# Ordering a fused attention and Fourier-mixing kernel anew: slots in twos, new durations in the order's model, an earlier copy of the mask factors

## The chip, the cores and the metric

The kernel runs on one core of one Trainium2 chip. The metric is the device time in microseconds (us) of one execution. "TensorE" is the matrix engine (PE in the profile, PEld its weight loads), "VectorE" is DVE, "ScalarE" is ACT, "GpSimd" is POOL and "SyncE" (SP) issues most of the DMAs (454 of the 459 in the profile before). PSUM is the memory of the four pools in which this kernel keeps TensorE's results; a "bank" is one result's room in such a pool.

## The reference

```python
# B, H, S, D = 4, 8, 768, 64; d_model = H*D = 512; blocks of 32
scores = scale * q @ k.T                       # per batch and head
mask = |blk_i - blk_j| <= 1  or first/last block  or 3 random blocks per row of blocks
attn = softmax(where(mask, scores, -1e9))      # + 1e-9 in the denominator
x = (attn @ v)  -> (B, S, 512)
mixed = real(fft(fft(x, axis=1), axis=2))
u = x + mixed
un = (u - mean) / sqrt(var + 1e-6)
out = u + relu(un @ w_ch1) @ w_ch2             # 512 -> 2048 -> 512
```

## The kernel before

Attention is worked in *units* of 128 keys by 384 queries for two heads. Two units are a *slot*; six slots make a pair of heads, 24 slots a batch, 96 slots the whole attention. A slot has scores S (TensorE), an Exp (ScalarE), the mask, values V (TensorE) and the sums of the softmax (additions on GpSimd, then a short matmul). The mask comes in two ways: as a product on VectorE, or, where VectorE is needed elsewhere, as a low-rank product on TensorE with two small *factors* that is added to the scores.

Between the slots of batch b lies what is left of batch b-1. First its *preparation* (`apart`): normalisation, folds of x on VectorE, the Fourier products `zp`, `pq` and `end` on TensorE, layer norm, transposes. Then its *channels* (`late`), the two large matrix products. The program is straight-line: when it is built, Python keeps a clock for each engine (`when`) and places each step where its modelled inputs are ready. A wrong duration there gives no wrong result, only another order.

```python
def keep_factors():                       # the factors' first room is needed for acc
    kept = room(2, [P, 2, S], "factors", BF16)      # room 2 of the weights' buffers
    for a, t in enumerate(factors["at"]):
        nc.sync.dma_start(out=kept[:, a, :], in_=t)
    factors["at"] = kept[:, 0, :], kept[:, 1, :]    # every later use reads the copy

def turn(n, a, half):                     # q (a=0) or k (a=1) of head pair n, transposed
    ...
    tag, pool = ("m", ps_m) if first and a == 0 else ("t", ps_t)   # m: 2 banks, t: 1 bank
    ...

def scores(us):
    for u in us:
        ...
        if n < NP or (factors["at"] and True):
            by_pe.add(u)                  # mask on TensorE
        for i in range(2):
            nc.tensor.matmul(s[:, i, 0:HS], kT[rows, ...], qT[rows, queries], ...)
    for u, s in got:                      # mask factors, only for units of by_pe
        ...

def weigh(u, s):                          # Exp, and the mask product where not by_pe
    ...
    if c > 0:
        acc_at[n, half] = busy("POOL", 2.0, e_at[u]) + HOP
    for i in range(2 if c > 0 else 0):
        nc.gpsimd.tensor_add(out=acc, in0=..., in1=e[:, i, :])

# preparation: (kind, what to do, modelled us on TensorE, ScalarE, VectorE)
def d(us, fn, *args):
    return "d", lambda: fn(*args), 0.0, 0.0, us
first = [d(1.8, fold_0, 0), d(1.8, fold_0, 1), d(1.0, fold_1, 0), d(0.9, fold_e),
         d(1.0, fold_1, 1), d(1.2, fold_2, 0), d(0.6, fold_2, 2), d(1.3, fold_2, 1)]
first += [("M" if g == 2 else "m", lambda g=g: along(g), 2.1, ...) for g in range(4)]   # zp
pq = [...]                                # across(m): pq, and for m == 1 also `end` in bank t

def gap(rest=0.0, ahead=None, kinds="tm"):
    while apart:                          # place preparation steps that fit here
        kind, fn, pe, act, dve, need = apart[0]
        ...
        if kind in "dw":                  # VectorE step: only if it ends soon enough
            if max(when["DVE"], state["ready"]) + dve > when["PE"] + rest + ahead:
                break
        elif kind != "-":                 # TensorE step: only if its input and bank are ready
            if max(state["ready"], bank_at) > when["PE"] + 0.1:
                break
        do_apart()
    ...

def begin(b):
    ...
    def go():                             # the end of the preparation
        late.extend(rest)                 # now there are channels
        factors["at"] = None              # and the mask goes back to VectorE

def slot(sl):
    for u, ps in scores(units):
        weigh(u, ps)
    if not late:
        gap(1.5)
    if 0 < sl <= B * SB:
        for u in done:                    # the units of the slot before
            values(u)
        if phase == 0 or sl == SB:
            add_up(done)
    ...                                   # loads, turns, sums, placing of x
    gap(max(state["owed"], 0.0))
    while late and state["owed"] >= late[0][1] / 2:
        state["owed"] -= late[0][1]
        channel_step()                    # C: 7 products (9 us) or one of 3.5 us
        gap(max(state["owed"], 0.0))
    ...
    if sl == SB - 3:
        keep_factors()
```

## Time and profile before

| kernel before | |
|---|---|
| median of 3 runs | 1087.49 us (1086.93 to 1092.15) |
| span of the profiled execution | 1090.0 us |
| TensorE busy | 1056.0 us, 97% |
| waits of TensorE over 0.15 us, sum | 21.5 us |
| time lost at half clock behind waits | 7.5 us |
| the rest of TensorE's stream | 1048.6 us |
| changes of TensorE's tile shape, 230 to 820 us | 164 |
| matmuls of mask factors | 172 |

The waits, the half clock and the rest of the stream are three parts of one budget of TensorE, worked out from the raw records of one profiled execution. The waits leave out the 2.6 us before the first matmul. The clock records say where half clock was granted, and half of the work done in it is counted as lost (an `o` group takes 2.83 us there, at 119.98, and 1.51 at full clock, at 499.69). The rest is TensorE's busy time less this loss. (What is missing to the span are those 2.6 us, 9.5 us after the last matmul, and 0.5 us of shorter gaps.)

The page's chain says that TensorE sets the end (88% of the chain), so a microsecond is won or lost mainly where TensorE waits, runs slowly, or has more to do. One more view matters for the new durations, the summary of GpSimd's additions in the kernel before (duration in ns: minimum/median/maximum):

```profile
L602 POOL TENSOR_TENSOR acc<-acc,e x192: 988/999/2521, 136.3 to 810.3; 128x384 f32<-128x384 f32 x192
```

A unit has two of these, so 2.0 us is the median and what the old model says. Single ones take 2.5 times as long (2521 ns for 999). VectorE's folds were longer too while GpSimd added: of two of the same size, `sa` at L767 took 1.34 us with GpSimd adding, `sd` at L772 0.55 with GpSimd idle.

The same kernel does not always take the same time. These are eleven executions of the kernel before on one chip, with the mean clock that was granted to TensorE (sorted by their time):

```
1084.22 0.997   1087.11 0.995   1087.74 0.994   1087.85 0.994   1087.86 0.994   1090.39 0.991
1090.51 0.991   1090.77 0.989   1091.29 0.989   1091.77 0.989   1092.05 0.989
```

Time follows the clock here, from 1084.22 us at 0.997 to 1092.05 at 0.989: the same order of work gets more or less half clock from one execution to the next.

### The profile page before, as it was taken

To read this page: it belongs to the slowest core of one execution; us is meant where nothing else is said; L and a number is where in the kernel's file an instruction comes from. 1 tells how busy PE (TensorE), PEld (TensorE's weight loads), DVE (VectorE), ACT (ScalarE), POOL (GpSimd) and SP (SyncE) were. 2 spreads that over 40 slices of the span, in tenths; PEclk is the share of its full clock that TensorE was granted. 3 is DMA by queue.
4 is the path that set the end of the run, shared out by engine and by line. 5 is a ranking of instruction groups with operands and counts; after the bars stand their busy time and mean duration, and the time that the engine had idled before them with its cause. 6 is when DMAs were issued, how large, how long until landed. Compare 5 with 4: busy or idle time off the path is not lost.

```text
span 1090.0 us, 12509 instructions
## 1 busy us (share of the span) xinstructions
PE 1056.0 (97%) x4410; PEld 538.6 (49%) x4410; DVE 648.6 (60%) x1203; ACT 378.8 (35%) x762; POOL 274.2 (25%) x302
## 2 busy tenths in 40 slices
PE   8999879999999999999999999999999999999996
PEld 4333335454444555443444555443344555568575
DVE  5899682664468255665577446555556355575663
ACT  5988644552331212343342302334230202220210
POOL 1000084852243001355455000344630001000000
PEclk9999899999999999999999999999999999999998
DMA  7757311110010001223211000212000001000001
GB/s 223 229 164 240 94 30 30 39 35 15 15 29 1 1 0 31 57 39 55 44 21 32 1 0 15 63 33 39 13 8 7 1 0 30 29 1 0 1 19 44
DMA packets 108483, 47.07 MB, mean 43 GB/s; under 512 B 95854, under 2 KB 101244, under 8 KB 108412
## 3 DMA queue, kind: packets, MB, share of 16 engines
q1 hardware_dynamic: 106524, 45.38, 16.4%
q10 hardware_dynamic: 1856, 0.79, 0.3%
q8 instruction: 37, 0.61, 0.2%
q14 instruction: 34, 0.28, 0.1%
q0 software_dynamic: 32, 0.01, 0.0%
HBM read 37.11 MB, written 6.29 MB: 40 GB/s over the span
## 4 chain that ended last, share of the span: by engine, by line
PE 88%; DVE 6%; ACT 2%; issue 1%; DMA 1%; SPq 1%; POOL 0%; DVEq 0%; ACTq 0%; POOLq 0%
PE y L1066 23%; PE z L1010 15%; PE s L565 11%; PE o L615 10%; PE yp L1010 8%; PE yy L1129 6%; PE xp L1010 4%; PE zp L823 2%; PE tp L498 1%; PE sp L681 1%; PE s L575 1%; PE utp L935 1%; PE zp L794 1%; SPq L653 1%; PE sp L695 1%
## 5 line engine op out<-in xcount | busy, mean ns | idle before, releaser
L602 POOL TENSOR_TENSOR acc<-acc,e 128x384 f32<-128x384 f32 x192 | 200.4, 1077 | 128.4 <-DVE e L590 118.8
L565 PE MATMUL s<-qT,kT 64*128 64x384 f32 x768 | 154.4, 517 | 5.3 <-DVE e L590 3.8
L615 PE MATMUL o<-e,vr 128*64 128x384 f32 x768 | 148.7, 509 | 0.0
L1069 DVE TENSOR_TENSOR x<-y,x 128x512 f32<-128x512 f32 x72 | 49.7, 691 | 147.8 <-PE y L1066 147.8
L1066 PE MATMUL y<-w_sb,hA 128*128 128x512 f32 x288 | 131.1, 598 | 1.7 <-ACT zs L825 1.7
L1066 PE MATMUL y<-w_sb,hB 128*128 128x512 f32 x288 | 129.0, 597 | 0.7 <-DVE x L1069 0.7
L590 DVE TENSOR_TENSOR e<-s,mask 128x768 f32<-128x768 f32 x106 | 96.3, 949 | 46.6 <-ACT s L588 44.9
L588 ACT ACTIVATE s<-s 128x768 f32<-128x768 f32 x106 | 80.3, 789 | 118.2 <-PE s L565 117.6
L602 POOL TENSOR_TENSOR acc<-e 128x384 f32<-128x384 f32 x48 | 49.9, 1061 | 237.6 <-ACT e L585 129.1
L565 PEld LDWEIGHTS s<-qT,kT 64*128 64x128 f32 x768 | 63.7, 186 | 80.4 <-issue 23.0
L1010 PE MATMUL z<-unT,t 128*128 128x384 f32 x256 | 93.0, 486 | 0.0
L1015 DVE TENSOR_TENSOR hA<-z,hA 128x384 f32<-128x384 f32 x64 | 35.7, 558 | 89.5 <-PE z L1010 88.7
L1066 PEld LDWEIGHTS y<-w_sb,hB 128*128 128x128 f32 x288 | 53.2, 190 | 67.6 <-issue 65.8
L615 PEld LDWEIGHTS o<-e,vr 128*64 128x64 f32 x768 | 47.4, 138 | 76.3 <-issue 72.3
L1066 PEld LDWEIGHTS y<-w_sb,hA 128*128 128x128 f32 x288 | 52.4, 190 | 65.7 <-issue 58.5
L886 POOL TENSOR_SCALAR st<-st 128x1 f32<-128x1 f32 x24 | 6.7, 280 | 280.6 <-DVE st L885 280.2
L585 ACT ACTIVATE e<-s 128x768 f32<-128x768 f32 x86 | 65.0, 812 | 28.0 <-PE s L575 26.6
L1019 ACT ACTIVATE hA<-hA 128x384 f32<-128x384 f32 x64 | 33.5, 523 | 117.8 <-DVE hA L1015 117.4
L1010 PEld LDWEIGHTS z<-unT,t 128*128 128x128 f32 x256 | 48.6, 190 | 33.9
L1019 ACT ACTIVATE hB<-hB 128x384 f32<-128x384 f32 x64 | 33.5, 523 | 86.5 <-DVE hB L1015 86.5
L1010 PE MATMUL xp<-unT,w_sb 128*128 128x384 f32 x128 | 47.7, 495 | 0.3 <-DVE x L1069 0.3
L1010 PE MATMUL yp<-unT,w_sb 128*128 128x384 f32 x128 | 46.9, 489 | 0.5 <-DVE un L859 0.5
(202 smaller groups left out, 1389.7 us busy)
## 6 DMA issues: line engine op xcount, KB each, us to landing
wraw<-in_moe_w_ch_dram SPq DMA_DIRECT2D x32, 512.0 KB
vr<-in_v_dram SPq DMA_DIRECT2D x30, 192.0 KB
qr<-in_q_dram SPq DMA_DIRECT2D x48, 64.0 KB
x<-oT SPq DMA_DIRECT2D x192, 12.0 KB
kr<-in_k_dram SPq DMA_DIRECT2D x14, 192.0 KB
qb<-in_q_dram SPq DMA_DIRECT2D x28, 96.0 KB
kb<-in_k_dram SPq DMA_DIRECT2D x28, 96.0 KB
out_dram<-x SPq DMA_DIRECT2D x16, 128.0 KB
```

Of the source, the lines that this page charges most:

```text
L565: nc.tensor.matmul(s[:, i, 0:HS], kT[rows, c * P:(c + 1) * P], qT[rows, queries], start=True, stop=u not in by_pe)
L585: nc.scalar.activation(out=e, in_=s[:, :, 0:HS], func=ACT.Exp, scale=scale)
L588: nc.scalar.activation(out=s[:, :, 0:HS], in_=s[:, :, 0:HS], func=ACT.Exp, scale=scale)
L590: nc.vector.tensor_tensor(out=e, in0=s[:, :, 0:HS], in1=m.broadcast_to([P, 2, HS]), op=ALU.mult)
L602: nc.gpsimd.tensor_add(out=acc, in0=e_of[u - 1][:, i, :] if c == 1 else acc, in1=e[:, i, :])
L615: nc.tensor.matmul(o[D * i:D * i + D, :], vt[:, i, c, :], e[:, i, :], start=(c == 0), stop=(c == C - 1))
L1010: nc.tensor.matmul(to, a[:, k, :], c[:, k, :], start=(k == 0), stop=(k == ND // 2 - 1))
L1015: tt(out=to, in0=ps, in1=a, op=ALU.add)
L1019: nc.scalar.activation(out=h, in_=h, func=ACT.Relu)
L1066: nc.tensor.matmul(y, hs[0, half][:, l, m * P:(m + 1) * P], w2_sb[:, 4 * r + l, :], start=(l == 0), stop=(l == 3))
L1069: nc.vector.tensor_tensor(out=x[:, m, :], in0=y, in1=x[:, m, :], op=ALU.add)
L1129: nc.tensor.matmul(ps, a[:, k, :], c[k // 2][:, k % 2, :] if isinstance(c, list) else c[:, k, :], start=(k == 0), stop=(k == 3))
```

## The change

The intent has four parts. (1) *Slots in twos*: once there are channels, two slots are worked as S V V S C C in place of S V C S V C, because TensorE loses time at each change of tile shape (0.18 us each in a steady slot of the kernel before). (2) *Durations*: folds are modelled longer where GpSimd is at work, and an addition pair on GpSimd at 2.9 us in place of 2.0. (3) *Factors*: they are copied two slots sooner, to take away TensorE's wait for the copy (3.4 us). (4) *Bank*: the second half of a later q is transposed in the pool of two banks. The core of the diff:

```diff
+    def turn_on(n, a, half):
+        return "m" if n > NP and (a, half) == (0, 1) else "t"
...
-        tag, pool = ("m", ps_m) if first and a == 0 else ("t", ps_t)
+        tag, pool = ("m", ps_m) if first and a == 0 or turn_on(n, a, half) == "m" else ("t", ps_t)
...
-            acc_at[n, half] = busy("POOL", 2.0, e_at[u]) + HOP
+            acc_at[n, half] = busy("POOL", 2.9, e_at[u]) + HOP
...
-            return "d", lambda: fn(*args), 0.0, 0.0, us
+            return "d" + "d" * OPS.get(fn, 0), lambda: fn(*args), 0.0, 0.0, us
+        OPS = {fold_0: 1, fold_1: 1, fold_e: 3, fold_2: 2}
...
+    def behind(kind):
+        at = max(when["DVE"], state["ready"])
+        return 0.75 * (len(kind) - 1) if when["POOL"] > at else 0.0
...                                       # in do_apart() and gap():
+                dve += behind(kind)
...                                       # in slot(sl):
+        opens = sl % 2 == 0
+        state["paired"] |= opens and len(late) > 0
+        paired = state["paired"]
...                                       # sum_up(): values (and sums) of the oldest slot of `due`
+        if paired and len(due) == 2 and due[0] % SP % T == T - 1:
+            sum_up()
+        got = scores(units) if sl < B * SB else ()
+        if paired and len(due) == 2:
+            sum_up()
+        for u, ps in got:
+            weigh(u, ps)
...
+        while due and (opens or not paired):
+            sum_up()
+        due.append(sl)
...
+        more = paired and opens and sl < B * SB
...
+        while not more and rest():
             state["owed"] -= late[0][1]
             channel_step()
...
-        if sl == SB - 3:
+        if sl == SB - 5:
             keep_factors()
```

`rest()` is the time that is owed to the channels, or 0 where none of their steps is due. Cut: loads and turns a slot later or sooner and a sum that is placed at once, which keep the pairs whole, and `gap`, which gets `rest()` for what is owed. No arithmetic is added or taken away, except that the mask may lie on TensorE for more or fewer units.

More of the change, by code (lines that the diff above doesn't have):

```diff
@@ L482 @@
     s_at, e_at, oT_at, acc_at = {}, {}, {}, {}
+    def turn_on(n, a, half):
+        return "m" if n > NP and (a, half) == (0, 1) else "t"
     def turn(n, a, half):
         t = loaded[n, a]
-        if half == 0:
+        first_of = (n, a) not in turned
+        if first_of:
             turned[n, a] = tp_p.tile([P, S], FP32, tag="qk"[a] + "T", name="qk"[a] + "T")
@@ L510, in turn @@
             give(at, end)
-        if half == 1:
+        if not first_of:
             flat = t.rearrange("p t r i d -> p (t r i d)" if a == 0 else "p c i d -> p (c i d)")
@@ L1207 @@
     W_PACE = 1.42
-    short, apart, late = deque(), deque(), deque()
-    state = {"w": 0, "got": 0, "owed": 0.0, "ready": 0.0}
+    short, apart, late, due = deque(), deque(), deque(), deque()
+    asked = set()
+    state = {"paired": False, "total": None, "w": 0, "got": 0, "owed": 0.0, "ready": 0.0}
     def channel_step():
         late.popleft()[0]()
+    def behind(kind):
+        at = max(when["DVE"], state["ready"])
+        return 0.75 * (len(kind) - 1) if when["POOL"] > at else 0.0
     def do_apart():
         kind, fn, pe, act, dve, _ = apart.popleft()
-        if kind in "dw":
+        if kind[0] in "dw":
+            dve += behind(kind)
             state["ready"] = busy("DVE", dve, rstd_at[0] if kind == "w" else state["ready"]) + HOP
@@ L1241, in gap @@
                 break
-            if kind in "dw":
+            if kind[0] in "dw":
+                dve += behind(kind)
                 if kind == "w" and rstd_at[0] > max(when["DVE"], when["PE"]) + 0.2:
@@ L1281, in begin, with rest, once @@
         apart.append(("-", go, 0.0, 0.0, 0.0, hold))
+    def rest():
+        return state["owed"] if late and state["owed"] >= late[0][1] / 2 else 0.0
+    def once(*of):
+        if of in asked:
+            return False
+        asked.add(of)
+        return True
     def w_loads():
@@ L1296, in slot, with sum_up @@
         units = range(SLOT * sl, SLOT * sl + SLOT)
-        if sl < B * SB:
-            for u, ps in scores(units):
-                weigh(u, ps)
-        if not late:
-            gap(1.5)
-        if 0 < sl <= B * SB:
-            done = [u - SLOT for u in units]
+        opens = sl % 2 == 0
+        state["paired"] |= opens and len(late) > 0
+        paired = state["paired"]
+        def sum_up():
+            at = due.popleft()
+            done = range(SLOT * at, SLOT * at + SLOT)
             for u in done:
                 values(u)
-            if phase == 0 or sl == SB:
+            if at < SB:
                 add_up(done)
@@ L1309, in slot @@
                 e_of.pop(u)
-        if s == 3 and n + 2 < len(pairs):
+        if paired and len(due) == 2 and due[0] % SP % T == T - 1:
[5 more added lines that the diff above has]
+            weigh(u, ps)
+        if not paired and not late:
+            gap(1.5)
+        while due and (opens or not paired):
+            sum_up()
+        due.append(sl)
+        if s >= (4 if paired else 3) and n + 2 < len(pairs) and (n + 2, 0) not in loaded:
             load_q(n + 2)
@@ L1315, in slot @@
         reuse = n % NP == 0 and phase >= 2
-        if sl > 0 and s == (5 if reuse else 3) and sl <= B * SB:
+        if s >= (5 if reuse else 3) and (n, 0) in oT_at and once(n):
             b, j = pairs[n]
@@ L1339, in slot @@
             short.append(("t", acc_at[n - 1, 1], lambda: total(n - 1)))
+            state["total"] = short[-1]
         if n + 1 < len(pairs):
-            for at, a, half in ((1, 0, 0), (2 if n > 0 else 3, 0, 1), (4, 1, 0), (5, 1, 1)):
-                if s == at and n + 1 < BY_VECTOR:
-                    short.append(("t", 0.0, lambda a=a, half=half: turn(n + 1, a, half)))
+            for at, a, half in ((1, 0, 0), (2 if n > 0 else 3, 0, 1),
+                                (3 if paired else 4, 1, 0), (5, 1, 1)):
+                if s >= at and n + 1 < BY_VECTOR and once(n + 1, a, half):
+                    short.append((turn_on(n + 1, a, half), 0.0,
+                                  lambda a=a, half=half: turn(n + 1, a, half)))
             if s == 1:
@@ L1357, in slot @@
         state["owed"] = min(state["owed"], pace) + pace if late else 0.0
-        gap(max(state["owed"], 0.0))
-        while late and state["owed"] >= late[0][1] / 2:
+        more = paired and opens and sl < B * SB
+        if not more:
+            gap(rest())
+        while not more and rest():
             state["owed"] -= late[0][1]
             channel_step()
-            gap(max(state["owed"], 0.0))
-        while short and (s in (2, 5) or len(short) > 1 or phase == 0 or r == 0):
+            gap(rest())
+        must = (3, 5) if paired else (2, 5)
+        if s == 1 and state["total"] in short:
+            short.remove(state["total"])
+            state["total"][2]()
+        while short and (not more or r == 0) and (s in must or len(short) > 1 or phase == 0 or r == 0):
             ready = [i for i in short if max(i[1], min(free[i[0]])) <= when["PE"] + 0.1]
-            if not ready and s not in (2, 5) and r > 0 and sl > 1:
+            if not ready and s not in must and r > 0 and sl > 1:
                 break
```

## The prediction

> **What bounds the kernel now.** I read the page first, then TensorE's waits, then its timeline. From the page, the busy times and the chain that ended last:
>
> ```profile
> PE 1056.0 (97%) x4410; PEld 538.6 (49%) x4410; DVE 648.6 (60%) x1203; ACT 378.8 (35%) x762; POOL 274.2 (25%) x302
> ...
> PE 88%; DVE 6%; ACT 2%; issue 1%; DMA 1%; SPq 1%; POOL 0%; DVEq 0%; ACTq 0%; POOLq 0%
> ```
>
> TensorE is busy 97% of 1090.0 us and holds 88% of the chain; the next engine is at 60%. Only three things can shorten the kernel: fewer TensorE waits (1090 - 1056 = 34 us idle in all, head and tail included), less half-speed clock after a wait, and a denser stream. TensorE's waits, by releaser:
>
> ```profile
> PE s L565 <- DVE e L590: 3.8, 3, 1.7
> PE zp L794 <- DVE sa L767: 3.6, 1, 3.6
> PE s L575 <- DMA factors<-at_q: 3.4, 1, 3.4
> PE tp L498 <- ACT qT L507: 3.4, 3, 1.1
> ```
>
> Each of the four is touched by the change. What a wait costs beyond itself is in TensorE's timeline:
>
> ```profile
> 113.40 1.62 PE L565 MATMUL s<-qT,kT 64*128 64x384 f32 x8 [0.36 <-ACT e L585]
> 118.39 0.82 PE L575 MATMUL s<-factors 64*128 64x384 bf16 x4 [3.37 <-DMA factors<-at_q]
> 119.15 0.90 PE L637 MATMUL xt<-ident,oT 128*128 128x128 f32 x3
> 119.98 2.83 PE L615 MATMUL o<-e,vr 128*64 128x384 f32 x8
> 122.74 1.36 PE L681 MATMUL sp<-e,pick 128*32 128x384 f32 x8
> ```
>
> The `o` group takes 2.83 us here and 1.51 elsewhere. The trace's clock records show half clock from 116.98 for 6.83 us; of that 118.39 to 123.81 was worked, so about 2.7 us were lost on top of 3.4. The zp wait has half clock from 161.36 for 6.83 us (3.4 lost), the `s` wait at 718.4 half clock for 3.4 us (1.7 lost).
>
> Density, in a steady slot late in the run (scores, values, one channel step):
>
> ```profile
> 499.69 1.51 PE L615 MATMUL o<-e,vr 128*64 128x384 f32 x8
> 501.13 3.70 PE L1066 MATMUL y<-w_sb,hA 128*128 128x512 f32 x8
> 504.76 1.56 PE L565 MATMUL s<-qT,kT 64*128 64x384 f32 x8
> 506.25 1.51 PE L615 MATMUL o<-e,vr 128*64 128x384 f32 x8
> ```
>
> From one `o` group to the next is 6.56 us, with no wait. In the raw starts, matmuls (or pairs of half-array ones) of 384 columns follow at 0.316 to 0.322 us, those of 512 at 0.429, but the first interval after and the last before a change of shape (64*128, 128*64, 128*128) is 0.05 to 0.10 longer. The three changes of a slot cost 0.546 us, **0.18 each**.
>
> [...] `sd` at L772 took 0.55 us with GpSimd idle, `sa` of the same size at L767 1.34 with GpSimd adding.
>
> **The change, part by part.** No arithmetic is removed; the order is.
>
> *Slots in twos.* In place of S V C, S V C (S scores, V values, C channels) a pair is S V V S C C: 4 changes of shape for 6, 5 where a half ends among the values in front (one pair in three). I counted 164 changes between 230 and 820 us. Channels begin in slot 42, some two slots later after the change (below), so 26 pairs to slot 96: 26 x 4 + 9 for half ends + 8 for the `sp` groups = 121. Saved: 43 x 0.18 = **-7.8 us**.
>
> What might come back: the second S needs the PSUM of the first freed. First unit scored at +0.75, Exp 0.8, mask product 0.95, hops 0.2: free at +2.7; the second unit at +3.65. TensorE returns at 1.49 + 2 x 1.44 = 4.4, so it hardly waits; where a half ends only one V lies between (2.93 and 3.68 us): a few tenths. A pair that gets no channel step (paying out what is owed twice as coarsely gives about one or two a batch) has the next S only 1.5 us after: a wait of 1 to 1.5 us. I take +3. The present waits of `s` (3.8 + 1.7 of half clock) mostly fall away, being between single slots without a channel. Sum **-1.5**, a choice.
>
> *Durations.* The order is built with modelled times. Vector's timeline of the first batch's folds:
>
> ```profile
> 147.12 2.44 DVE L746 TENSOR_TENSOR sa<-x 128x1536 f32<-128x1536 f32 x1
> 149.48 2.55 DVE L746 TENSOR_TENSOR sd<-x 128x1536 f32<-128x1536 f32 x1
> 151.96 1.75 DVE L750 TENSOR_TENSOR sa<-sa 128x765 f32<-128x765 f32 x1
> 153.63 1.21 DVE L757 TENSOR_TENSOR e<-x 128x255 f32<-128x255 f32 x1
> ```
>
> Old model 1.8, 1.8, 1.0 (and 0.9 for the three of `e`, really 3.2); new, with GpSimd ahead, 2.55, 2.55, 1.75, 3.15. Through fold_2 the old sum falls some 5 us short, which is why `zp` was placed 3.64 + 0.71 us too soon. With the new sum it is placed about two slots later and scores and values fill the time: -4.35 and -3.4 of half clock, **-7.75**. Two more slots use the mask on TensorE (L575, 0.4 a slot): **+0.8**.
>
> *Bank for q's second half.* From batch 1 on it goes to another PSUM bank, so two of the three `tp` waits of 1.1 go: **-2.2**.
>
> *Factors two slots sooner.* The intent is to remove the wait of 3.4. But the copy is moved, and its first use moves with it: from slot 22 to slot 20. The room it copies into belongs to the rounding of weight chunk 26 until that is done, and that is issued in slot 19 itself. Vector is behind:
>
> ```profile
> 109.79 0.69 DVE L461 TENSOR_TENSOR w_sb<-w_sb,wraw 128x512 f32<-128x512 f32 x1
> ...
> 114.31 0.55 SPq L478 DMA_DIRECT2D factors<-at_k  x1
> 114.91 0.60 SPq L478 DMA_DIRECT2D factors<-at_q  x1
> ```
>
> Counting the L461 of the weights from 0, the one that ends at 110.48 is number 26 (26 mod 6 rooms = room 2). In the old order the copy stood behind six q loads and began at 114.31; in the new it can begin at about 110.5, 3.8 us sooner. It lands 3.44 us after its second issue, so at about 114.5. TensorE wants it in slot 20, whose scores start at 104.52, so at 105.9: it waits 8.6 us in place of 3.4. Half clock follows either. **+5.2 us.** The part that is meant to help makes its wait longer.
>
> Sum: -7.8 - 1.5 - 7.75 + 0.8 - 2.2 + 5.2 = -13.3; 1087.5 - 13.3 = 1074.2, and I say **1074**.
>
> **Rivals.** (a) *The copy's wait vanishes*: were the room free earlier than I count, 3.4 + 2.7 would be saved in place of 5.2 lost, 11 us better: about 1063, over 2%. Against it: the count of L461, and that a DMA into a buffer still in use would be a race. (b) *The pairs stall*: if the second S waits for `e L590` in most pairs, for 0.5 to 1 us, the 26 pairs lose 13 to 26 us: 1085 to 1095. For it: the window is 4.4 us against a need of 3.65, and Vector sometimes enters with transposes (1.53 us) or quad additions in front; against it, the program's own clock tracks these, and V's inputs are always a pair old. (c) *Batch 0's folds end in another wait*: the norm scaling (6.24 us for six, modelled 5.4) stays under-modelled, so a stall of a microsecond or two may stay, and with it half clock: +3 to +5. (d) *Loads of q a slot later* are hidden anyway: used two slots later, some 12 us. Nothing there.
>
> **Range and chances.** The parts are uncertain by about 3 (pairs), 3 (zp), 2 (copy) and 4 (new waits), some 6 in all; with rivals (a) and (b) at about 15% each I take 1065 to 1084. Over 2% faster means below 1065.7: mostly (a), 0.14. Over 2% slower, above 1109, needs a wait in every pair of 1.5 us: 0.01.
>
> **What would show it.** Changes of shape between 230 and 820 near 121; `s <- e` among TensorE's waits under 4 us; no `zp <- sa` wait; one or no `tp <- qT` wait after 100 us; a wait of L575 for `factors` of 7 to 10 us, beginning near 106. If that last wait is gone, my count of the room is wrong; if `s L565` waits over 10 us, the window between the two scores is.

## The result

The changed kernel takes 1096.72 us (median of 4 runs, 1095.12 to 1097.39; the kernel before in the same rounds 1088.81). The result is correct. The ratio is 1.0067, with a 95% interval of 1.0038 to 1.0097: **slower by 0.7%**, some 7.3 us. Every ratio in this document is the mean time of one kernel's fast runs over the mean of the fast runs of the kernel before in the same rounds, so it is not quite the ratio of the medians quoted. A difference of ratios times 1087.5 us gives the microseconds below.

From the page of the changed kernel, its busy line and its chain by engine:

```profile
PE 1050.5 (96%) x4434; PEld 542.2 (50%) x4434; DVE 648.8 (59%) x1191; ACT 378.2 (35%) x762; POOL 274.4 (25%) x302
...
PE 88%; DVE 5%; ACT 2%; issue 2%; DMA 1%; POOL 1%; SPq 1%; ACTq 0%; DVEq 0%; POOLq 0%
```

TensorE still sets the end. It is busy for 5.5 us less, and the span (1094.7) is 4.7 longer than the 1090.0 of before: it idles more. It also has 24 matmuls more. TensorE's waits, with releaser, sum, number and longest:

```profile
PE s L580 <- DMA factors<-at_q: 8.9, 1, 8.9
PE end L839 <- DVE sums L670: 5.4, 1, 5.4
PE s L570 <- DVE e L595: 2.8, 2, 2.0
...
PE y L1074 <- DVE x L1077: 2.5, 3, 1.8
PE sp L700 <- ACT x L643: 2.2, 1, 2.2
PE xp L1018 <- DVE x L1077: 2.2, 2, 1.8
...
PE tp L503 <- ACT qT L512: 1.1, 1, 1.1
```

The four waits of before that the prediction named have changed as it said: the factors' wait has grown to 8.9 us, `zp <- sa` is gone, `s <- e` is down to 2.8, and one wait of 1.1 us is left for `tp`. But waits stand there that it did not have, above all `end <- sums`, 5.4 us.

TensorE's timeline around the copied factors (start, duration, line, product, count, wait):

```profile
103.72 1.56 PE L570 MATMUL s<-qT,kT 64*128 64x384 f32 x8
114.20 0.82 PE L580 MATMUL s<-factors 64*128 64x384 bf16 x4 [8.93 <-DMA factors<-at_q]
114.96 2.83 PE L620 MATMUL o<-e,vr 128*64 128x384 f32 x8
```

The group of matmuls with factors takes 0.82 us here and 0.49 at 120.72, the `o` group 2.83 here and 1.51 at 514.14: the clock is at half from 108.4 for 10.24 us. Half clock was also granted from 166.48 for 3.41 us, with a wait of 2.21 us (`sp`, ended at 166.80), and not with one of 1.97 us (`s`, ended at 444.69). SyncE issued the two copies at 109.71 and 110.28, against 114.31 and 114.91 before.

A pair in the steady part, with no wait in it:

```profile
501.37 1.56 PE L570 MATMUL s<-qT,kT 64*128 64x384 f32 x8
502.86 2.80 PE L620 MATMUL o<-e,vr 128*64 128x384 f32 x16
505.59 1.56 PE L570 MATMUL s<-qT,kT 64*128 64x384 f32 x8
507.08 7.13 PE L1074 MATMUL y<-w_sb,hA 128*128 128x512 f32 x16
514.14 1.51 PE L620 MATMUL o<-e,vr 128*64 128x384 f32 x8
```

S V V S C C takes 514.14 - 501.37 = 12.77 us, against 2 x 6.56 = 13.12 for two single slots before: 0.35 us for two changes of shape, as counted. The budgets (one profiled execution each; lost at half clock varies as said above):

| | waits | half clock | rest of stream | changes of shape, 230 to 820 us | mask matmuls | span |
|---|---|---|---|---|---|---|
| before | 21.5 | 7.5 | 1048.6 | 164 | 172 | 1090.0 |
| after | 31.8 | 6.7 | 1043.8 | 142 | 196 | 1094.7 |

The denser stream is worth 4.8 us, and 10.3 us of new waits have taken its place. The first channel product is at 260.39 us, against 230.6 before: slot 48 in place of 42.

### The profile page after: what moved, and what is told of

The parts are those of the page before. It is cut to its first block, busy times and chain, and to the rows that moved or that the text cites.

```text
span 1094.7 us, 12542 instructions
## 1 busy us (share of the span) xinstructions
PE 1050.5 (96%) x4434; PEld 542.2 (50%) x4434; DVE 648.8 (59%) x1191; ACT 378.2 (35%) x762; POOL 274.4 (25%) x302
## 4 chain that ended last, share of the span: by engine, by line
PE 88%; DVE 5%; ACT 2%; issue 2%; DMA 1%; POOL 1%; SPq 1%; ACTq 0%; DVEq 0%; POOLq 0%
PE y L1074 22%; PE z L1018 15%; PE s L570 11%; PE o L620 11%; PE yp L1018 7%; PE yy L1137 6%; PE xp L1018 3%; PE zp L828 2%; PE tp L503 1%; PE sp L686 1%; PE s L580 1%; PE zp L799 1%; POOL acc L607 1%; PE sp L700 1%; PE utp L943 1%
## 5 line engine op out<-in xcount | busy, mean ns | idle before, releaser
L620 PE MATMUL o<-e,vr 128*64 128x384 f32 x768 | 144.4, 504 | 0.0
L595 DVE TENSOR_TENSOR e<-s,mask 128x768 f32<-128x768 f32 x94 | 85.5, 950 | 55.4 <-ACT s L593 52.1
L593 ACT ACTIVATE s<-s 128x768 f32<-128x768 f32 x94 | 71.3, 791 | 84.9 <-PE s L570 84.6
L590 ACT ACTIVATE e<-s 128x768 f32<-128x768 f32 x98 | 74.4, 815 | 44.3 <-PE s L580 36.3
L1038 ACT COPY hA<-xp 128x384 f32<-128x384 f32 x32 | 15.3, 478 | 116.9 <-PE xp L1018 116.9
```

The source lines that it names most:

```text
L590: nc.scalar.activation(out=e, in_=s[:, :, 0:HS], func=ACT.Exp, scale=scale)
L593: nc.scalar.activation(out=s[:, :, 0:HS], in_=s[:, :, 0:HS], func=ACT.Exp, scale=scale)
L595: nc.vector.tensor_tensor(out=e, in0=s[:, :, 0:HS], in1=m.broadcast_to([P, 2, HS]), op=ALU.mult)
L620: nc.tensor.matmul(o[D * i:D * i + D, :], vt[:, i, c, :], e[:, i, :], start=(c == 0), stop=(c == C - 1))
```

## The experiments

Twelve kernels ran; all gave correct results. They undo one part of the change, do one part alone, or try a version that the former ones point to.

### The copy back in slot 21 (copy_late)

```diff
-        if sl == SB - 5:
+        if sl == SB - 3:
             keep_factors()
```

> The changed kernel with the factors copied in slot 21 again, as before the change; all else stays. Theory (the copy's first use moved with it, so TensorE waits 8.9 us instead of 3.4, on top of everything else): the wait of the mask matmuls for factors is back to 3.3 to 3.6 us, in slot 22, and the kernel gains about 5.5 us on the changed one: ratio to the kernel before near 1.0015, about 1091 us. Rival (slot 20's wait only takes work out of a later wait, such as that of the end product of the first batch): no gain, ratio stays near 1.0067, and the 5.4 us wait of the end product grows.

Measured: 1090.36 us, ratio 1.0016 (0.9999 to 1.0033). Against the change this is 0.0051, or 5.5 us, better. TensorE's waits:

```profile
PE end L839 <- DVE sums L670: 5.4, 1, 5.4
PE s L580 <- DMA factors<-at_q: 3.9, 1, 3.9
```

The factors' wait falls from 8.9 to 3.9; nothing else near the top moves. This step of the prediction (+5.2 us) was right in its size too.

### The old durations (old_durations)

```diff
-            acc_at[n, half] = busy("POOL", 2.9, e_at[u]) + HOP
+            acc_at[n, half] = busy("POOL", 2.0, e_at[u]) + HOP
...
-        OPS = {fold_0: 1, fold_1: 1, fold_e: 3, fold_2: 2}
+        OPS = {}
```

> The changed kernel with the old modelled durations (folds without the addition for GpSimd, 2.0 us an addition); pairs and early copy stay. Theory (the new durations only moved the wait and put off the channels): the zp wait of 3.6 + 0.7 us is back, the waits of sp (2.2) and of the end product (5.4) go, channels begin in slot 43 instead of 48, five slots fewer use the mask on TensorE (about 2 us), and the kernel gains 4 to 8 us on the changed one: ratio near 1.001. Rival (the new durations do what they are for, some 7.75 us): it loses 3 to 8 us, ratio 1.010 to 1.014.

Measured: 1089.95 us, ratio 1.0021 (1.0002 to 1.0039): 0.0046, or 5.0 us, *better* without the new durations. The waits that changed:

```profile
PE s L580 <- DMA factors<-at_q: 8.8, 1, 8.8
PE zp L799 <- DVE sa L772: 5.2, 1, 5.2
```

The wait of `zp` is back, 5.2 us, and the kernel is faster all the same, because `end <- sums` and `sp <- x` are gone. Channels begin in slot 43 in place of 48, with 176 mask matmuls for 196. A group of four of these is 0.42 us from start to start in the stream, so 20 more are 2.1 us; the rest of the stream is 1041.5 for 1043.8. Waits are 29.1 for 31.8, and half clock 4.1 for 6.7.

Where does the wait of `end` come from? In the changed kernel TensorE needs the one bank of pool t. VectorE has to empty it first, with the `sums` of L670:

```profile
206.10 0.39 PE L841 MATMUL pq<-cd_sb,zc 128*128 128x128 f32 x2
211.90 0.59 PE L839 MATMUL end<-cd_sb,zc 128*1 128x129 f32 x2 [5.41 <-DVE sums L670]
```

VectorE's timeline of the same stretch:

```profile
205.49 1.22 DVE L903 TENSOR_SCALAR un<-x,st 128x512 f32<-128x512 f32 x1 [4.73 <-POOL st L893]
206.64 2.34 DVE L878 TENSOR_TENSOR x<-x,un 128x255 f32<-128x255 f32 x2
...
211.22 0.18 DVE L890 BATCH_NORM_AGGREGATE st<-st 128x2 f32<-128x6 f32 x1
211.32 0.53 DVE L670 TENSOR_TENSOR sums<-sp,sums 128x384 f32<-128x384 f32 x1
```

VectorE waited 4.73 us for a layer-norm value from GpSimd (`st`, L893), and `sums` stood behind that in its queue, and behind another 5.8 us of VectorE's own work (205.49 to 211.32). GpSimd's timeline:

```profile
202.54 1.96 POOL L607 TENSOR_TENSOR acc<-e 128x384 f32<-128x384 f32 x2 [5.78 <-PE sp L700]
...
204.89 0.57 POOL L893 TENSOR_TENSOR st<-st,neg_half 128x1 f32<-128x1 f32 x1
```

GpSimd waited 5.78 us until TensorE had read the accumulator (`sp`, L700, at 201.51), and the value for VectorE stood behind this addition. So TensorE's own late `sp` comes back to TensorE through GpSimd and VectorE. In the kernel before, `end` had no wait:

```profile
195.58 0.38 PE L834 MATMUL end<-cd_sb,zc 128*1 128x129 f32 x2
```

The four waits in a row are read from the trace; that the new durations bring them about is shown by this run, where they are gone.

### Which of the two durations (pool_back, folds_back)

pool_back has only the first of the two edits above (2.9 back to 2.0), folds_back only the second (`OPS = {}`).

> The changed kernel with an addition on GpSimd modelled at 2.0 us again; the folds keep their new durations, pairs and early copy stay. Theory A (the 2.9 us do the harm: they make the order hold back the whitening steps, so that channels begin in slot 48): channels begin in slot 45, three slots fewer use the mask on TensorE (1.2 us), the wait of the end product (5.4 us, and about 2.9 us of half clock) is gone: 6 to 9 us better than the changed kernel, ratio 0.998 to 1.001. Theory B (the longer folds do the harm): the wait of 5.4 us stays, at most 2 us better, ratio 1.005.

> The changed kernel with the old modelled folds and the addition at 2.9 us; pairs and early copy stay. Theory A (the 2.9 us do the harm): the zp wait of 3.6 to 5.2 us and its half clock are back and the later waits stay: 2 to 6 us worse than the changed kernel, ratio 1.009 to 1.012. Theory B (the folds do the harm): 4 to 6 us better, ratio near 1.002.

Measured: pool_back 1094.64 us, ratio 1.0071 (1.0052 to 1.0090), no different from the change. folds_back 1090.51 us, ratio 1.0032 (1.0014 to 1.0051), 0.0035 or 3.8 us better. Against the change, from other rounds, this difference lies at the edge of the noise; against pool_back, from the same rounds, it is clear (1089.29 to 1091.37 us for 1093.31 to 1095.83). The waits of pool_back, then of folds_back:

```profile
PE s L580 <- DMA factors<-at_q: 9.0, 1, 9.0
PE end L839 <- DVE sums L670: 5.4, 1, 5.4
```

```profile
PE s L580 <- DMA factors<-at_q: 8.6, 1, 8.6
PE zp L799 <- DVE sa L772: 5.2, 1, 5.2
```

It is the longer folds that trade the wait of `zp` for that of `end`. The longer additions are without measurable effect where the folds are long.

### `end` in another bank (end_other_bank)

If the shared bank were the cause, `end` could go to the pool of two banks.

```diff
-                end = ps_t.tile([P, 512], FP32, tag="t", name="end")
+                end = ps_m.tile([P, 512], FP32, tag="m", name="end")
...
-                give(bank("t"), when["PE"] + 2.0)
+                give(bank("m"), when["PE"] + 2.0)
```

> The changed kernel with the end product of the Fourier step (one row, in the middle of the second block's products) written to a bank of the two-bank pool that the block itself uses, no longer to the one bank that the sums of the additions share; all else stays. Theory (the folds' new place puts the end product right behind the sums, in a bank that VectorE empties 5 us later; the order's model does not know that the step needs that bank): the wait of 5.4 us at 206 us is gone, and the half clock behind it (6.8 us long, 2.9 lost): 5 to 8 us better than the changed kernel, ratio 0.999 to 1.002. Rival (VectorE is simply late there, so the next product waits as long): 0 to 2 us better, ratio 1.005 or more.

Measured: 1098.49 us, ratio 1.0089 (1.0070 to 1.0108), no gain. Its timeline, in which `end` has no wait:

```profile
205.56 0.38 PE L839 MATMUL end<-cd_sb,zc 128*1 128x129 f32 x2
...
211.04 0.91 PE L503 MATMUL tp<-ident,qr 128*128 128x128 f32 x4 [4.02 <-DVE sums L670]
```

The wait only moves to the next user of the bank. What is late is VectorE's `sums`; that `end` shares its bank decides only who waits for it.

### The durations without pairs (durations_only, no_pairs)

durations_only is the kernel before with the new durations of the folds and additions alone. no_pairs is the change without `state["paired"] |= opens and len(late) > 0`, so that no slot is ever paired.

> The kernel before with the new modelled durations alone: no pairs, copy in slot 21, old bank. Theory (without the pairs the longer modelled folds leave the third batch's preparation unfinished when the channel steps of the second run out, as in the run without pairs): the zp wait is gone, waits of 5.4 us (end product) and of 7 us or so (transposes of the whitened rows, near 720 us) come instead: 15 to 28 us slower than the kernel before, ratio 1.014 to 1.026. Rival (the loss of the run without pairs came from the early copy or the bank): ratio 0.995 to 1.005.

> The changed kernel with the slots never paired; new durations and early copy stay. Theory (a pair saves 0.36 us of shape changes, at 24 pairs some 7 to 8 us, less 3 to 5 us of new waits for additions and products on VectorE in the pairs): it loses 3 to 6 us on the changed one, ratio 1.010 to 1.012. Rival (the pairs stall as much as they save): same as the changed one, or faster.

Measured: durations_only 1117.92 us, ratio 1.0287 (1.0265 to 1.0309); no_pairs 1121.42 us, ratio 1.0304 (1.0280 to 1.0329). Both are far slower than the change, and nothing in the prediction has room for it. (The expectation for no_pairs missed it too: a loss of 3 to 6 us on the change was expected, and it is 0.0237 or 25.8 us.) Waits of TensorE in durations_only:

```profile
PE s L570 <- DVE e L595: 10.4, 8, 2.6
PE utp L943 <- ACT x L643: 7.2, 1, 7.2
...
PE end L839 <- DVE sums L670: 5.4, 1, 5.4
```

and its timeline where they arise:

```profile
704.91 7.13 PE L1074 MATMUL y<-w_sb,hB 128*128 128x512 f32 x16
711.88 0.60 PE L943 MATMUL utp<-ident,un 128*128 128x128 f32 x4
...
725.34 1.11 PE L943 MATMUL utp<-ident,un 128*128 128x128 f32 x4 [7.20 <-ACT x L643]
726.38 2.83 PE L620 MATMUL o<-e,vr 128*64 128x384 f32 x8
...
754.98 1.78 PE L570 MATMUL s<-qT,kT 64*128 64x384 f32 x8 [2.62 <-DVE e L595]
```

After the channel group at 704.91 no channel product comes until 766.12. The channels of one batch have run out before the next batch's preparation is through, and scores and values alone do not cover the mask products on VectorE and the transposes. (ScalarE's `x` at 724.80, which ends the wait of 7.20, itself had waited 9.93 us for the store of an earlier x.) In the built program, 30 steps of the third batch's preparation are left after the channel steps of slot 77, which have to be placed before a buffer is used again; in the change, and in the kernel before, it is 13. The third batch's channels begin in slot 90 in both kernels without pairs, and in slot 79 in those two. So the new durations push the preparation back, and without pairs the third batch's falls off an edge. With pairs they cost 5.0 us, without them 31 us (0.0287 x 1087.5). Why pairs leave fewer steps over was not tried by itself.

### The pairs alone (pairs_only)

The kernel before with the pairs, and with none of the other three parts.

> The kernel before with the pairs alone (old durations, copy in slot 21, old bank for the second half of q). Theory: about 120 changes of shape between 230 and 820 us instead of 164, 43 x 0.18 = 7 to 8 us of denser stream, up to 3 us of it lost to waits: ratio 0.993 to 0.996, 1080 to 1084 us. Rival (pairs gain nothing): 0.998 to 1.002.

Measured: 1084.44 us, ratio 0.9963 (0.9938 to 0.9988): 4.0 us faster. Its budget: waits 24.0 (21.5 before), rest of the stream 1042.0 (1048.6), changes of shape 132 (164). So 6.6 us of stream are won, which is 0.2 for each of the 32 changes saved, and waits take 2.5 us more, as the net of several (0.8 of it is the wait for the factors, 4.2 for 3.4). 6.6 - 2.5 = 4.1 is close to the measured 4.0. (The profiled span is 8.2 us shorter, but 4.1 of that is less half clock in that execution.) Two of the waits that the kernel before did not have at this size:

```profile
PE xp L1018 <- DVE x L1077: 4.0, 3, 1.8
...
PE z L1018 <- DVE hA L1023: 2.0, 1, 2.0
```

The longest two waits of `xp`, of 1.8 us each, end at 447.75 and 698.95. There the last channel step of one batch is followed by the first step of the next, with nothing but transposes between: the second starts before VectorE has emptied its bank. In the kernel before, scores and values stood between the two at that place, and `xp <- x` came to 0.3 us. So this is a price of channel steps in a row. The wait of `z` ends at 307.69, inside a single channel step, and was not followed further. The waits of `s` on `e`, 3.8 us before, are down to 0.8 here: the window between the two scores holds.

### The copy early, its first use late (pairs_split)

pairs_only with the copy in slot 19, but read from slot 23 only:

```diff
-        factors["at"] = kept[:, 0, :], kept[:, 1, :]
+        factors["kept"] = kept[:, 0, :], kept[:, 1, :]
...
+        if sl == SB - 1 - 1:
+            factors["at"] = factors["kept"]
```

> The kernel before with the pairs, and with the factors copied in slot 19 but read from slot 23 on (in the change they are read from slot 20 on); old durations, old bank. Theory (the harm of the early copy is the early first use, not the early copy): no wait for factors at all, neither 8.9 nor 3.4 us, and no half clock after it: 4 to 7 us better than the kernel with the pairs alone, ratio 0.989 to 0.993, about 1078. Rival (the copy itself is slow, or the queue, whenever it is issued): a wait of 3 us or more stays, ratio 0.996.

Measured: 1078.15 us (1076.77 to 1078.60), ratio 0.9919 (0.9901 to 0.9938): 0.0044, or 4.8 us, better than pairs_only, and **0.8% faster than the kernel before**. The first use of the copy:

```profile
118.83 0.49 PE L580 MATMUL s<-factors 64*128 64x384 bf16 x4
```

No wait, and full clock. SyncE issued the copies at 109.54 and 110.12, as early as in the change. So the early copy did no harm here; what hurt was that its first use moved with it, by the one line that switches the readers over at once. Whether the copy has to be early at all was not tried: in pairs_only, with the copy in slot 21, the factors were there at 118.60, and the first use here is at 118.83, so the late use alone may have been enough, though barely.

### The bank (bank_back, pairs_bank_split)

bank_back is the change with `turn_on` always returning "t". pairs_bank_split is pairs_split with the change's bank for q.

> The changed kernel with the second half of q back in the old bank; pairs, early copy and new durations stay. Theory (the prediction's: the new bank takes two waits of 1.1 us away): two or three more waits of tp for qT of 1.1 us after 130 us, 2 to 4 us slower than the changed kernel, ratio 1.008 to 1.010. Rival (the sum of the other runs, which leaves the bank nothing: early copy 5.5, durations 5.0, pairs -4): same as the changed kernel within 1.5 us.

> pairs_split (pairs, old durations, copy in slot 19 but first used in slot 23; 0.9919 [0.9901, 0.9938], 1078.15 us) with one thing more: the second half of q goes to the two-bank pool, as the change has it. Theory A: the bank is worth what its waits are: the tp <- qT waits of 1.1 us (three in the kernel before, four in bank_back) fall to the single one at 17 us, nothing takes their place, and the time falls by 2 to 4 us: ratio 0.988 to 0.990, about 1075 us. Rival B: the two-bank pool has other users at those places (sums of the first batch, Fourier products, channels), so that the waits come back under another name or as later placing: ratio 0.991 to 0.994, 1077 to 1081 us, with waits of TensorE on that pool that pairs_split has not.

Measured: bank_back 1099.13 us, ratio 1.0089 (1.0069 to 1.0109). Its interval overlaps that of the change (1.0038 to 1.0097), so the 2.4 us between the ratios are not clear. The waits do come back: `tp <- qT` has five in place of one. pairs_bank_split 1080.65 us, ratio 0.9923 (0.9900 to 0.9946), the same as pairs_split. The waits of pairs_split, then of pairs_bank_split:

```profile
PE zp L799 <- DVE sa L772: 3.6, 1, 3.6
PE tp L503 <- ACT qT L512: 3.4, 3, 1.1
```

```profile
PE zp L799 <- DVE sa L772: 5.2, 1, 5.2
...
PE tp L503 <- ACT qT L512: 1.1, 1, 1.1
```

Two waits of 1.1 us are gone. One of them lay ahead of `zp`, and the wait of `zp` grew by 1.5: TensorE comes sooner to a place where VectorE is not ready yet. Two more short `tp` waits (0.7 and 0.6) came as well. Here the bank is worth nothing that can be measured.

### The best version (best_d)

The split copy, pairs, the long folds, additions at 2.0 us, `end` in the pool of two banks, and the old bank for q.

> A candidate: the pairs, the factors copied in slot 19 and read from slot 23 on, the new durations of folds with additions at 2.0 us, the end product in the two-bank pool, old bank for q. Theory (with the early first use and the shared bank mended, the durations earn what they are for): no waits for factors, zp or the end product; 2 to 5 us better than the pairs with the late first use (ratio 0.9919), ratio 0.987 to 0.990. Rival (the later start of the channels, three slots more with the mask on TensorE, and the sp wait of 2.2 us eat it): ratio 0.991 to 0.994.

Measured: 1079.85 us (1078.12 to 1080.20), ratio 0.9913 (0.9893 to 0.9932), which the intervals cannot tell from pairs_split. One of its waits of TensorE:

```profile
PE sp L700 <- POOL acc L607: 2.3, 1, 2.3
```

Neither `zp` nor `end` is among its waits any more; its waits are 18.2 us for the 19.8 of pairs_split, with this new wait of `sp` among them. But its stream is 4.1 us longer (1045.5 for 1041.4): 12 mask matmuls more (184 for 172) are 1.3 us of that, and the rest was not followed. The long folds can be had without harm then, but not with a gain. Why no `tp` waits for `sums` here, as one did in end_other_bank, was not pursued.

## Why the prediction was wrong

It said 1074.2, and the change measures 1096.7: -13.3 predicted, +7.3 by the ratio.

| step | predicted us | measured us | from |
|---|---|---|---|
| copy two slots sooner | +5.2 | +5.5 | change against copy_late |
| pairs | -7.8 - 1.5 | -4.0 | pairs_only |
| durations | -7.75 + 0.8 | +5.0 | change against old_durations |
| bank | -2.2 | 0 to -2.4, not clear | bank_back, pairs_bank_split |

The measured parts come to between +4.1 and +6.5, so 1 to 3 us of the +7.3 are not accounted for; parts of an order do not add up exactly.

**The step that failed is "Durations"**: "With the new sum it is placed about two slots later and scores and values fill the time: -4.35 and -3.4 of half clock". The first half came true: the wait of `zp` went. The second did not. In old_durations TensorE came to `zp` at 165.43 - 5.16 = 160.3 us; in the change it comes at 175.1, 14.8 us later: 34 slots have been scored by then for 31, so it was placed three slots later, not two:

```profile
165.43 2.94 PE L799 MATMUL zp<-cs_sb,sa 128*128 128x385 f32 x4 [5.16 <-DVE sa L772]
```

```profile
175.07 1.56 PE L799 MATMUL zp<-cs_sb,sa 128*128 128x385 f32 x4
```

All that follows `zp` moves with it: six more slots without channels for two assumed, 24 more mask matmuls (about 2.5 us for the 0.8 written down), and above all another meeting of the engines around 205 us, where `end` waits 5.4 us. In place of -6.95 us, the durations cost +5.0. Beyond two slots of mask, the prediction looked only at the wait that the new number removes. (That wait's half clock was also a little over-read: of the 6.83 us from 161.36, 0.7 were idle, so 3.1 us were lost, not 3.4.) It named the right doubt as rival (c), a wait elsewhere and half clock for +3 to +5, but as a remainder of `zp`, and gave it no weight in the sum. Removing the wait that VectorE set on TensorE did not make VectorE faster: `sa` released `zp` at 165.43 us in old_durations and was done at 165.86 in the change, and TensorE was only elsewhere meanwhile.

**Pairs** were right in mechanism: 0.2 us of stream won for each change of shape saved, 0.18 predicted. The term mis-sized is that for new waits: -1.5 predicted, +2.5 in the trace of pairs_only. The prediction examined the window between the two scores, which held, and did not examine channel steps in a row. Fewer changes were saved too: 32 for 43.

**The copy** was right in direction, size and cause: a wait of 8.93 us, from 105.3 on, against 8.6 from 105.9. It also rejected its own rival (a) rightly. **The bank** is supported where the waits are counted in the change, and worth nothing in pairs_split.

Nearly every sign that the prediction wanted to see in the new profile was there, `zp` and `s` and `tp` and factors, and still the sum had the wrong sign. Only the changes of shape missed theirs, 142 for 121. The late start of the channels explains some 10 of these 21 (pairs_only, with channels from slot 42, has 132); the others were missing from the count. The signs tested each part where it acts; none asked what the same order would do 40 us later.

## What to carry to other kernels

In an order built from modelled durations, a better number need not give a better order (the new durations cost 5.0 us here): before taking a longer duration, follow what is placed after it, to the next buffer or queue that the delayed engine holds, and try it alone and undone. Here the wait for a copy hung on when its result was first read as much as on when it was issued (8.9 us when read from slot 20, none when read from slot 23, with the two runs' copies issued within 0.2 us), so move the two apart. When work is grouped to save switching, look for the new waits in every group, also in those that the saving was not about (in pairs_only they took 2.5 of the 6.6 us saved).
